# Merging the two rounds of the 32x32-tile transforms into one six-bank group, and kept sums in half banks

## The chip, the cores and the metric

The kernel runs on one core of a Trainium2 chip: TensorE (PE, with its weight loads listed apart as PEld), VectorE (DVE), ScalarE (ACT), GpSimd (POOL) and SyncE (SP, whose work here is to issue DMAs), with eight PSUM banks of 128 partitions x 512 float32 values between TensorE and the others. The metric is the time of one execution on the device in microseconds, the median of several runs.

## The reference

The input x has 2048 rows of 640 values (bfloat16). It is normalised row by row; the normalised rows go two ways, through a filter in the frequency domain and through a two-layer perceptron, and both results are added to x:

```
xn  = (x - mean(x)) / sqrt(var(x) + 1e-5)          # per row
F   = irfft2(rfft2(xn) * (w_r + i*w_i))            # 2048 x 321 weights
M   = gelu(xn @ w1 + b1) @ w2 + b2                 # 640 -> 1536 -> 640
out = x + F + M
```

## The kernel before

Everything is matrix multiplication on TensorE, the Fourier transforms too: a two-dimensional transform is cut into short transforms that are products with small constant tables (gtab, etab, mtab on the way in, ntab, getab, htab on the way out).

**The filter's way.** x is loaded as 16 chunks of 128 rows, normalised, and turned (chunks 0 to 3 by TensorE, 4 to 15 by transposing DMAs on SP) into xnT. Stage A multiplies folded rows with gtab, the b groups multiply with etab and leave Xb. Stage **C** finishes the forward transform along the rows with products of 32x32: for each P of 0 to 3 (two pairs of row blocks), two rounds r, each of 32 matmuls of 32x322 (Xb with mtab). The sixteen 32x32 tiles of the array work side by side, each on its own 32 rows and 32 columns; the two halves v = 0, 1 (real and imaginary) are accumulated on each other. A round fills four banks, which two copies of 644 columns empty into Y, one for each pair. DVE multiplies Y with the weights (L841, T<-Y,Wf) and adds the parts (L845, Z<-T). Stage **D** goes back: for each P, two rounds v, each of 32 matmuls of 32x320 (Z with ntab) into four banks. Each pair's two banks are emptied by a copy of 512 and one of 128 columns, which read PSUM at every second column and write U. Transposing DMAs (L866) turn U into XV again; stage E (getab) and the last products (htab) follow, with unfolding adds on DVE between them (L896, L901).

**The perceptron's way.** The first layer (xnT,W1, listed as xnT,W) is worked in six blocks of chunks, twelve column blocks of w1 each; ACT applies gelu (L774) into gT. The second layer (W2,gT, listed as W,gT) needs twelve products per chunk. For nine of the sixteen chunks (KEEP) these are made early: two banks collect twelve times 512 + 128 columns, and one DVE add of 640 (L948) puts them into an f32 store, which already holds b2 (L924) and x (an accumulating DMA on POOL, L942). At the end DVE adds the filter's result to it (L957) and the rows go out. The other chunks make the second layer at the end, in the same banks as the htab products.

**Order.** The sequence of operations on every engine is written out in a table (ORDER, one list of operation numbers per engine). Within an engine the program runs in that order; an engine waits by semaphores for results of others, and TensorE doesn't wait for itself: sync() leaves those waits out (`d.eng != o.eng or o.eng != "pe"`). ZONE says in which of the eight PSUM banks each kind of product may be put; a group can start when all of its banks have been emptied. So between two groups of C or D, TensorE works on first- and second-layer matmuls in the banks left over. All matmuls are issued by one helper, so they have the line L550; ACT's copies have L561 and DVE's L562, after the helper `copy`. The groups are told apart by their operands.

## Time and profile before

| | us |
|---|---|
| median of 3 runs | 146.68 (146.58 to 147.81) |
| span of the profiled execution, first to last instruction | 144.9 |
| TensorE busy in it | 141.2 |
| VectorE busy | 112.2 |
| ScalarE busy | 79.5 |
| GpSimd busy | 23.8 |

Beside the span no time is listed for the whole of the profiled execution; the runs' median lies 1.8 us above the span. In a row of the profile, "L550 PE MATMUL ps<-Xb,mtab 32*32 32x322 bf16 x32" is 32 matmuls of line 550 on TensorE in tiles of 32x32, with 322 columns each. In the timeline the first number is the start in us from the span's start, the second the time from the first start to the last end of the row's instructions; what stands in brackets is the idle time of the engine before the row and what ended it. In the groups of instructions the two numbers behind the first bar are the total busy time in us and the mean length of one in ns; lengths of pipelined matmuls overlap each other.

### The profile page before, as it was taken

Reading aid. Unit: us, or ns where it says so; the run is one execution under the profiler, and the core shown is the slowest. Engines: PE = TensorE matmul, PEld = TensorE weight load, DVE = VectorE, ACT = ScalarE, POOL = GpSimd, SP = SyncE. Lnnn points to the kernel's source line nnn. Section 1 sums busy time; section 2 is a strip of 40 time slices with the busy share of each in tenths; the row PEclk is TensorE's granted clock in tenths of the full one; section 3 lists DMA queues with packets and bytes.
Section 4 is the critical chain, followed back from the end, with each engine's and each line's share of the span. In section 5 each row is a group of like instructions: output and inputs, shape, how many; then the busy total and the mean of one; then the engine's idle time right before and its main releaser. Section 6 shows DMA issues by size and latency. Waiting matters only on the chain.

```text
span 144.9 us, 4085 instructions
## 1 busy us (share of the span) xinstructions
PE 141.2 (97%) x1720; PEld 90.6 (63%) x1720; DVE 112.2 (77%) x235; ACT 79.5 (55%) x145; POOL 23.8 (16%) x40
## 2 busy tenths in 40 slices
PE   7899999999999999999999999999999999999994
PEld 7799998987455464457554645554446666656573
DVE  1999999999843459799866967992432998998984
ACT  3219999999989668762455633216376755201000
POOL 2331302206100018220200120000054700000000
DMA  4998998987999736948767561362459895103225
GB/s 117 340 410 321 339 164 255 160 146 202 212 301 168 186 59 129 241 104 170 153 179 127 59 144 42 46 142 59 91 112 216 180 209 187 52 5 136 93 106 165
DMA packets 30841, 23.63 MB, mean 163 GB/s; under 512 B 20456, under 2 KB 26856, under 8 KB 30696
## 3 DMA queue, kind: packets, MB, share of 16 engines
q1 hardware_dynamic: 28432, 17.81, 50.5%
q0 software_dynamic: 2368, 5.57, 17.7%
q8 instruction: 13, 0.21, 0.6%
q14 instruction: 4, 0.03, 0.1%
q10 hardware_dynamic: 24, 0.00, 0.0%
HBM read 13.54 MB, written 2.62 MB: 112 GB/s over the span
## 4 chain that ended last, share of the span: by engine, by line
PE 94%; DMA 2%; DVE 2%; issue 0%; ACT 0%
PE ps L550 94%; DMA X<-in_A_x_dram 2%; DVE stats L670 1%; PE ps L714 1%; DVE mv L672 0%; ACT xnT L561 0%; DVE W L957 0%; DVE T L695 0%
## 5 line engine op out<-in xcount | busy, mean ns | idle before, releaser
L550 PE MATMUL ps<-W,gT 128*128 128x512 bf16 (+3 forms) x396 | 58.7, 295 | 0.0
L550 PE MATMUL ps<-xnT,W 128*128 128x256 bf16 (+2 forms) x384 | 58.4, 300 | 0.1
L550 PEld LDWEIGHTS ps<-W,gT 128*128 128x128 bf16 x396 | 30.3, 98 | 23.5 <-issue 1.6
L550 PEld LDWEIGHTS ps<-xnT,W 128*128 128x128 bf16 x384 | 33.3, 98 | 15.7 <-issue 1.6
L774 ACT ACTIVATE gT<-ps,b1col 128x256 bf16<-128x256 f32 (+1 forms) x72 | 35.4, 558 | 6.9 <-PE ps L550 6.5
L670 DVE BATCH_NORM_STATS2 stats<-X 128x6 f32<-128x320 bf16 x32 | 13.9, 476 | 2.1 <-DMA X<-in_A_x_dram 2.1
L561 ACT ACTIVATE Wf<-ps 128x960 bf16<-128x960 f32 (+1 forms) x8 | 7.0, 901 | 13.5 <-PE ps L550 13.5
L942 POOL DMA_DIRECT2D X<-in_A_x_dram x8 | 7.1, 1100 | 39.7 <-DMA Wf<-in_A_w_r_dram 17.1
L841 DVE TENSOR_TENSOR T<-Y,Wf 128x1288 bf16<-128x1288 bf16 x16 | 12.7, 826 | 0.0
L942 POOL DMA_DIRECT2D xnT<-in_A_x_dram x8 | 7.6, 1193 | 25.1 <-ACT xnT L924 25.1
L674 POOL TENSOR_TENSOR rstd<-mv,mhalf 128x2 f32<-128x2 f32 (+1 forms) x10 | 7.1, 714 | 26.6 <-DVE mv L672 26.4
L562 DVE CAST Y<-ps 128x644 bf16<-128x644 f32 x8 | 6.5, 828 | 5.5 <-PE ps L550 5.5
L561 ACT ACTIVATE Xb<-ps 128x960 bf16<-128x960 f32 (+1 forms) x7 | 6.0, 857 | 7.3 <-PE ps L550 7.3
L561 ACT ACTIVATE XV<-ps 128x1280 bf16<-128x1280 f32 (+3 forms) x10 | 9.5, 963 | 0.7 <-PE ps L550 0.7
L562 DVE CAST Xb<-ps 128x960 bf16<-128x960 f32 (+1 forms) x5 | 5.5, 1092 | 4.3 <-PE ps L550 4.2
L730 DVE TENSOR_TENSOR T<-T 128x512 bf16<-128x512 bf16 (+1 forms) x32 | 8.5, 312 | 0.0
L695 DVE TENSOR_SCALAR T<-X,mv,rstd 128x640 bf16<-128x640 bf16 (+2 forms) x17 | 7.1, 430 | 0.9 <-POOL rstd L674 0.6
L896 DVE TENSOR_TENSOR Wf<-Wf 128x960 bf16<-128x960 bf16 (+1 forms) x12 | 7.0, 597 | 0.5 <-ACT Wf L561 0.3
L957 DVE TENSOR_TENSOR W<-ps,X 128x640 bf16<-128x640 f32 x8 | 6.5, 820 | 1.1 <-PE ps L550 1.1
L561 ACT ACTIVATE U<-ps 128x512 bf16<-128x512 f32 (+1 forms) x10 | 3.8, 434 | 6.2 <-PE ps L550 6.2
L845 DVE TENSOR_TENSOR Z<-T 128x644 bf16<-128x644 bf16 x16 | 7.2, 489 | 0.1
L957 DVE TENSOR_TENSOR W<-ps,xnT 128x640 bf16<-128x640 f32 (+2 forms) x10 | 6.7, 686 | 0.7 <-PE ps L550 0.7
(55 smaller groups left out, 135.4 us busy)
## 6 DMA issues: line engine op xcount, KB each, us to landing
X<-in_A_x_dram POOLq DMA_DIRECT2D x8, 320.0 KB, 5.2
xnT<-in_A_x_dram POOLq DMA_DIRECT2D x8, 320.0 KB, 5.1
out_dram<-W SPq DMA_DIRECT2D x15, 160.0 KB, 1.8
X<-in_A_x_dram SPq DMA_DIRECT2D x7, 320.0 KB, 6.7
W<-in_B_w_dram SPq DMA_DIRECT2D x5, 384.0 KB, 5.2
W<-in_B_w_dram SPq DMA_DIRECT2D x4, 480.0 KB, 7.2
Wf<-in_A_w_i_dram SPq DMA_DIRECT2D x6, 160.5 KB, 5.4
Wf<-in_A_w_r_dram SPq DMA_DIRECT2D x6, 160.5 KB, 4.0
```

The costliest lines, as they stand in the source:

```text
L550: ins = e.matmul(o_, lhsT=lw, rhs=rh, start=st, stop=sp_, skip_group_check=True)
L561: return e.activation(dst(), src(), ACT.Copy, scale=scale)
L562: return e.tensor_copy(dst(), src())
L670: st_op[c] = K.op([("dve", 0.393)], pr, lambda e, _, c=c, h=h: e.bn_stats(stats[:, c, 6 * h:6 * h + 6], view(X, c * D + H2 * h, [[1, H2]]) ...
L674: K.op([("pool", 0.65)], 500, lambda e, _, a=a, b=b: e.tensor_tensor(out=rstd[:, a:b], in0=mv[:, a:b, 1], in1=mhalf[:, a:b], op=ALU.pow), ...
L695: o = K.op([("dve", 0.066 + (d1 - d0) / 1980.0)], pr, lambda e, _, c=c, n=n, xnv=xnv, d0=d0, d1=d1: e.tensor_scalar(out=xnv(n, d0, [[1, d1 ...
L730: ring_ops.append(K.op([("dve", dve_us(4 * w, 2))], pr, lambda e, _, op=op, x1v=x1v, xfv=xfv, o_=o_, o0=o0, o1=o1, w=w: e.tensor_tensor(ou ...
L774: K.op([("act", act_us(128 * nt, 1))], pr + PRIO["gelu"] + GP[bi], lambda e, _, c0=c0, nt=nt, fc=fc, hps=hps, at=at: e.activation(gT[:, fc ...
L841: filt_ops.append(K.op([("dve", dve_us(4 * KP, 2))], pr, lambda e, _, k=k, Y=Y, TB=TB, pair=pair: e.tensor_tensor(out=view(TT, TB.slot * 8 ...
L845: K.op([("dve", dve_us(2 * KP, 2))], pr, lambda e, _, TB=TB, Z=Z, r=r, op=op: e.tensor_tensor(out=view(Zb, Z.slot * 4 * KP + r * KP, [[2 * ...
L942: xo_ops[c] = K.op([("pool", 0.9)], 51 - c / 20, lambda e, _, c=c, xov=xov: e.dma_start(xov(0, D), xv[:, c, :], accum_op=ALU.add), reads=[ ...
L957: K.op([("dve", dve_us(w))], 95, lambda e, _, os_=os_, fps=fps, o0=o0, w=w, xov=xov, base=base: e.tensor_tensor(out=view(W1, OST + os_.slo ...
```

## The change

1. **C:** both rounds of a P are one group of six banks. It is issued as three lists of 24, 48 and 24 matmuls (64 of 161 columns and 32 of 322). The second list follows the first at once. The third writes into the banks 0 and 1 again, behind what the first list put there, and so its first instruction waits on a semaphore until the first list is through (`hard`: the one case in which TensorE waits for itself). Three copies empty the group: 644 columns (of both pairs), 966 and 966.
2. **D:** both rounds of a P are one group of six banks, 128 matmuls of 32x160 in lists of 32, 64 and 32, the third waiting as above. The moving operand is every second element of Z, so that the result stands contiguously in PSUM. The group is emptied in three operations: 256 + 64 columns for each of the two pairs, 768 + 192 for the second pair, and 768 + 192 for the first.
3. **Kept sums:** in two halves of 320 columns, each in one bank, with twelve matmuls of 320 and a DVE add of 320 each.
4. **Banks and order:** ZONE gives C and D the banks 0 to 5 or 2 to 7, the first layer prefers banks 6 and 7, then 4 and 5. The table ORDER is new on every engine.

The number of columns that TensorE streams in C, D and the second layer is the same as before. The core of the diff, without the tables:

```diff
--- before.py
+++ after.py
...
-        o.alts, o.alt = alts, None
+        o.alts, o.alt, o.hard = alts, None, ()
-            o.waits = [d for d in set(o.deps) if d.nbytes or d.eng != o.eng or o.eng != "pe"]
+            o.waits = [d for d in set(o.deps) if d.nbytes or d.eng != o.eng or o.eng != "pe" or d in o.hard]
...
-ZONE = {"hps": [(4, 8)], "bps": [(0, 4)], "cps": [(0, 4)], "dps": [(0, 4)],
-        "eps": [(0, 4)], "fin": [(4, 8), (0, 4)], "fps": [(4, 8)], "tps": ANY, "aps": ANY}
+ZONE = {"hps": [(6, 8), (4, 6), (0, 4)], "bps": [(0, 4), (4, 8)], "cps": [(0, 6), (2, 8)], "dps": [(0, 6), (2, 8)],
+        "eps": [(0, 4), (4, 8)], "fin": [(4, 8), (0, 4)], "fps": [(6, 8), (4, 6), (0, 4)], "tps": ANY, "aps": ANY}
-CHAIN = "b1 b0 c01 c00 b2 c10 d01 c11 d00 b4 b3 d10 d11 c20 c21 b5 c30 d20 d21 c31 d30 d31".split()
+CHAIN = "b1 b0 c0 b2 c1 d0 b4 b3 d1 c2 b5 c3 d2 d3".split()
...
+        def chained(lists, prio, reads, ps):
+
+            a = pe([("small", 0.147)], prio, lists[0], reads=reads, writes=[ps])
+            b = pe([("small", 0.294)], prio + 5, lists[1], reads=reads, writes=[ps], gate=[a])
+            c = pe([("small", 0.188)], prio + 6, lists[2], reads=reads, writes=[ps], gate=[b], after=[a])
+            c.hard = [a]
+            return c
+
...
-            for r in range(2):
-                cps = Buf(f"cps{P}_{r}", psum, 4, ZONE["cps"])
-                zone[f"c{P}{r}"] = pe([("small", 0.335)], PRIO["pc"] - P / 2 + 0.02 * r, lambda P=P, r=r, cps=cps: [
-                    (psb(cps.slot + 2 * pp + hi, [[1, KP]], 0, 64 * qq + 32 * (lo ^ pp), 32),
-                     part(mtab, 64 * hi + 32 * lo, 32, (P == pp == qq == hi == lo == 0) * 128 + v * 64 + r * 32, [[1, 32]]),
-                     part(xb3, 64 * hi + 32 * lo, 32, xb_at[4 * P + 2 * pp + qq]() + v * KP, [[1, KP]]), v == 0, v == 1)
-                    for v in range(2) for pp, qq, hi, lo in tiles],
-                    reads=in_xb + [B_xbpad, B_m], writes=[cps])
-                for pp, Y in enumerate(Ys):
-                    K.op([("act", act_us(644)), ("dve", dve_us(644))], PRIO["pc"] - two[pp] / 5,
-                         copy(lambda Y=Y, r=r: view(Yb, Y.slot * 4 * KP + r * KP, [[2 * KP, 2], [1, KP]]),
-                              lambda cps=cps, pp=pp: psb(cps.slot + 2 * pp, [[512, 2], [1, KP]])), reads=[cps], writes=[Y])
+            cps = Buf(f"cps{P}", psum, 6, ZONE["cps"])
+            KH = KP // 2
+
+            def ctile(pp, r, v, k0, k1, bank, at, P=P, cps=cps):
+                return [(psb(cps.slot + bank + hi, [[1, k1 - k0]], at, 64 * qq + 32 * (lo ^ pp), 32),
+                         part(mtab, 64 * hi + 32 * lo, 32, (P == pp == qq == hi == lo == 0) * 128 + v * 64 + r * 32, [[1, 32]]),
+                         part(xb3, 64 * hi + 32 * lo, 32, xb_at[4 * P + 2 * pp + qq]() + v * KP + k0, [[1, k1 - k0]]), v == at == 0, v == 1)
+                        for _, qq, hi, lo in tiles[:8]]
+            zone[f"c{P}"] = chained([
+                lambda t=ctile: t(0, 0, 0, 0, KH, 0, 0) + t(1, 0, 0, 0, KP, 2, 0) + t(0, 0, 1, 0, KH, 0, 0),
+                lambda t=ctile: t(0, 0, 0, KH, KP, 4, 0) + t(1, 0, 1, 0, KP, 2, 0) + t(0, 0, 1, KH, KP, 4, 0) + t(0, 1, 0, 0, KP, 4, KH) + t(1, 1, 0, 0, KH, 2, KP) + t(1, 1, 1, 0, KH, 2, KP),
+                lambda t=ctile: t(0, 1, 1, 0, KP, 4, KH) + t(1, 1, 0, KH, KP, 0, KH) + t(1, 1, 1, KH, KP, 0, KH)],
+                PRIO["pc"] - P / 2, in_xb + [B_xbpad, B_m], cps)
+            ya, yb = Ys
+            for n, bufs, dst, src in (
+                    (644, Ys, lambda ya=ya, yb=yb: view(Yb, ya.slot * 4 * KP, [[2 * KP, 2], [(yb.slot - ya.slot) * 4 * KP + KP + KH, 2], [1, KH]]), lambda cps=cps: psb(cps.slot, [[512, 2], [KH, 2], [1, KH]])),
+                    (966, [yb], lambda yb=yb: view(Yb, yb.slot * 4 * KP, [[2 * KP, 2], [1, KP + KH]]), lambda cps=cps: psb(cps.slot + 2, [[512, 2], [1, KP + KH]])),
+                    (966, [ya], lambda ya=ya: view(Yb, ya.slot * 4 * KP + KH, [[2 * KP, 2], [1, KP + KH]]), lambda cps=cps: psb(cps.slot + 4, [[512, 2], [1, KP + KH]]))):
+                K.op([("act", act_us(n)), ("dve", dve_us(n))], PRIO["pc"] - P / 2, copy(dst, src), reads=[cps], writes=bufs)
 
...
-            for v in range(2):
-                dps = Buf(f"dps{P}_{v}", psum, 4, ZONE["dps"])
-                d_ops.append(pe([("small", 0.335)], PRIO["ipc"] - P / 2 + 0.02 * (1 - v), lambda P=P, v=v, Zs=Zs, dps=dps: [
-                    (psb(dps.slot + 2 * pp + qq, [[1, H2]], 0, 64 * hi + 32 * lo, 32),
-                     part(ntab, 64 * qq + 32 * (lo ^ pp), 32, (P == pp == qq == hi == lo == 0) * 96 + 32 * ((0, 2), (1, 0))[v][r], [[1, 32]]),
-                     part(Zb, 64 * qq + 32 * (lo ^ pp), 32, Zs[pp].slot * 4 * KP + (2 * hi + r) * KP + v, [[1, H2]]), r == 0, r == 1)
-                    for r in range(2) for pp, qq, hi, lo in tiles], reads=Zs + [B_n], writes=[dps]))
-                zone[f"d{P}{v}"] = d_ops[-1]
-                for pp, U in enumerate(Us):
-                    def evac(e, name, U=U, v=v, uv=uv, dps=dps, pp=pp):
+            dps = Buf(f"dps{P}", psum, 6, ZONE["dps"])
+
+            def dtile(pp, q, r, bank, at, P=P, Zs=Zs, dps=dps):
+                return [(psb(dps.slot + bank + qq, [[1, Q4]], at * Q4, 64 * hi + 32 * lo, 32),
+                         part(ntab, 64 * qq + 32 * (lo ^ pp), 32, (P == pp == qq == hi == lo == 0) * 96 + 32 * ((0, 2), (1, 0))[q // 2][r], [[1, 32]]),
+                         part(Zb, 64 * qq + 32 * (lo ^ pp), 32, Zs[pp].slot * 4 * KP + (2 * hi + r) * KP + q // 2 + q % 2, [[2, Q4]]), r == at == 0, r == 1)
+                        for _, qq, hi, lo in tiles[:8]]
+            d_ops.append(chained([
+                lambda t=dtile: t(0, 0, 0, 0, 0) + t(1, 0, 0, 2, 0) + t(0, 0, 1, 0, 0) + t(1, 0, 1, 2, 0),
+                lambda t=dtile: [x for k in range(2) for r in range(2) for x in t(0, 1 + k, r, 4, k) + t(1, 1 + k, r, 2, 1 + k)],
+                lambda t=dtile: [x for r in range(2) for x in t(0, 3, r, 4, 2) + t(1, 3, r, 0, 1)]],
+                PRIO["ipc"] - P / 2, Zs + [B_n], dps))
+            zone[f"d{P}"] = d_ops[-1]
+            for own in ((0, 0), (1, 3)), ((1, 0),), ((0, 1),):
+                many = 3 if len(own) == 1 else 1
+
+                def evac(e, name, own=own, many=many, Us=Us, uv=uv, dps=dps):
+                    for pp, q in own:
                         for o_, w in ((0, 128), (512, 32)):
-                            ins = copy(lambda: uv(U, o_ + 2 * w * v, [[D, 2], [w, 2], [1, w]]), lambda: psb(dps.slot + 2 * pp, [[512, 2], [1, 2], [2, w]], o_ // 2))(e, name)
-                        return ins
-                    K.op([("act", act_us(512) + act_us(128)), ("dve", dve_us(512) + dve_us(128))], PRIO["ipc"] - two[pp] / 5, evac,
-                         reads=[dps], writes=[U, B_us[pp]], after=a_ops + ring_ops)
+                            ins = copy(lambda: uv(Us[pp], o_ + w * q, [[D, 2], [w, many], [1, w]]), lambda: psb(dps.slot + (0 if many == 1 else 4 - 2 * pp), [[512, 2], [Q4, many], [1, w]], o_ // 4 + Q4 * (q == 3)))(e, name)
+                    return ins
+                K.op([("act", len(own) * (act_us(256 * many) + act_us(64 * many))), ("dve", len(own) * (dve_us(256 * many) + dve_us(64 * many)))], PRIO["ipc"] - P / 2, evac,
+                     reads=[dps], writes=[x for pp, _ in own for x in (Us[pp], B_us[pp])], after=a_ops + ring_ops)
...
                 if kept:
-                    kps = Buf(f"kps{c}", psum, 2, ZONE["fps"])
-                    second(c, kps, 0, D, pr, ([kept_ops[-2]] if len(kept_ops) > 1 else []) + [l1_of[j][-1] for j, (t0, nt) in enumerate(BLOCKS) if t0 <= c < t0 + nt])
                     xo1, xo = xo, Buf(f"xk{c}")
-                    kept_ops.append(K.op([("dve", dve_us(D))], 30, lambda e, _, kps=kps, xov=xov: e.tensor_tensor(
-                        out=xov(0, D), in0=psb(kps.slot, [[1, D]]), in1=xov(0, D), op=ALU.add), reads=[kps, xo1], writes=[xo]))
+                    for o0 in (0, H2):
+                        kps = Buf(f"kps{c}_{o0}", psum, 1, ZONE["hps"])
+                        second(c, kps, o0, H2, pr, ([kept_ops[-2]] if len(kept_ops) > 1 else []) + [l1_of[j][-1] for j, (t0, nt) in enumerate(BLOCKS) if t0 <= c < t0 + nt], base=lambda o0: o0)
+                        kept_ops.append(K.op([("dve", dve_us(H2))], 30, lambda e, _, kps=kps, xov=xov, o0=o0: e.tensor_tensor(
+                            out=xov(o0, H2), in0=psb(kps.slot, [[1, H2]]), in1=xov(o0, H2), op=ALU.add), reads=[kps, xo1], writes=[xo]))
```

How the order stands now at three places. First, TensorE at the first group of C (Xb,mtab; etab,XV are the b groups, xnT,W1 the first layer, W2,gT the second). Before:

```order
L550 MATMUL ps<-xnT,W1 128x512 x5
L550 MATMUL ps<-Xb,mtab 32x322 x32
L550 MATMUL ps<-xnT,W1 128x512 x2
L550 MATMUL ps<-W2,gT 128x512
L550 MATMUL ps<-W2,gT 128x128
L550 MATMUL ps<-W2,gT 128x512
L550 MATMUL ps<-W2,gT 128x128
L550 MATMUL ps<-W2,gT 128x512
L550 MATMUL ps<-W2,gT 128x128
L550 MATMUL ps<-Xb,mtab 32x322 x32
L550 MATMUL ps<-xnT,W1 128x512 x3
```

The two rounds stand apart, with 2 first-layer matmuls and 3 pairs of the second layer between them. The same place in the changed kernel, from the second half of the first merged group to the b group that follows:

```order
L551 MATMUL ps<-Xb,mtab 32x161 x8
L551 MATMUL ps<-Xb,mtab 32x322 x8
L551 MATMUL ps<-Xb,mtab 32x161 x16
L551 MATMUL ps<-Xb,mtab 32x322 x8
L551 MATMUL ps<-Xb,mtab 32x161 x16
L551 MATMUL ps<-W2,gT 128x320 x3
L551 MATMUL ps<-xnT,W1 128x512 x5
L551 MATMUL ps<-W2,gT 128x320 x3
L551 MATMUL ps<-etab,XV 128x160 x24
```

The 64 matmuls of two rounds have become 96 narrower ones in one run (40 more of them stand ahead of these rows), and eleven matmuls stand between the group and the next b group.

Second, TensorE at the first group of D (Z,ntab) of the changed kernel:

```order
L551 MATMUL ps<-W2,gT 128x320 x15
L551 MATMUL ps<-xnT,W1 128x512 x10
L551 MATMUL ps<-Z,ntab 32x160 x128
L551 MATMUL ps<-W2,gT 128x320 x21
L551 MATMUL ps<-etab,XV 128x160 x24
```

Before, two groups `Z,ntab 32x320 x32` stood at different places there, with first- and second-layer matmuls and a group of C between them; now 128 matmuls stand in one run and 21 of the second layer behind them.

Third, the queue of POOL from the first rstd on (rstd is the scale of the normalisation, Wf the filter's weights). Before:

```order
L674 TENSOR_TENSOR rstd<-mv,mhalf 128x1 x2
L674 TENSOR_TENSOR rstd<-mv,mhalf 128x2 x3
L571 MEMSET Xb 128x6x3
L674 TENSOR_TENSOR rstd<-mv,mhalf 128x2 x2
L545 DMA Wf<-in_A_w_i_dram 16x5136
L674 TENSOR_TENSOR rstd<-mv,mhalf 128x2
L545 DMA Wf<-in_A_w_r_dram 16x5136
```

And now:

```order
L675 TENSOR_TENSOR rstd<-mv,mhalf 128x1
L574 MEMSET Wf 128x2
L675 TENSOR_TENSOR rstd<-mv,mhalf 128x1 x2
L546 DMA Wf<-in_A_w_i_dram 16x5136
L546 DMA Wf<-in_A_w_r_dram 16x5136
L675 TENSOR_TENSOR rstd<-mv,mhalf 128x2 x6
```

Both loads of filter weights have moved ahead of all six rstd of two chunks, and the clearing of Xb to the front of the program.

## The prediction

> **What bounds the kernel now.** First the page: how much of the span each engine works, and how evenly.

> ```profile
> span 144.9 us, 4085 instructions
> PE 141.2 (97%) x1720; PEld 90.6 (63%) x1720; DVE 112.2 (77%) x235; ACT 79.5 (55%) x145; POOL 23.8 (16%) x40
> PE   7899999999999999999999999999999999999994
> PE 94%; DMA 2%; DVE 2%; issue 0%; ACT 0%
> ```

> TensorE is busy for 97% of the span, in every slice but the first two and the last, and the chain that ended last is 94% TensorE. The chain of waits tells whether it is one unbroken run:

> ```profile
> 11.67 131.12 PE ps L550 x1598
> 142.78 0.02 issue
> 142.81 0.33 DVE W L957
> ```

> It is: from 11.67 to 142.78 us each matmul is released by the matmul before it. So only what changes the time of the matmul stream moves the end, or what opens a gap in it. Busy is not the same as streaming columns, though, so I look for matmuls that come apart further than their columns explain. The pitch first, from the timeline at two plain places:

> ```profile
> 108.07 1.79 PE L550 MATMUL ps<-W,gT 128*128 128x512 bf16 x12
> 109.70 0.59 PE L550 MATMUL ps<-xnT,W 128*128 128x512 bf16 x2
> ...
> 141.71 0.99 PE L550 MATMUL ps<-W,gT 128*128 128x160 bf16 x12
> 142.54 0.23 PE L550 MATMUL ps<-Wf,htab 128*128 128x160 bf16 x1
> ```

> Twelve matmuls (six of 512 and six of 128 columns) take 109.70 − 108.07 = 1.63 us, 0.272 for 640 columns, 0.425 ns a column; twelve of 160 columns take 0.83, 0.069 each, 0.43 ns a column. Now the timeline around one group of 32x32 tiles in C, then in D:

> ```profile
> 75.15 0.81 PE L550 MATMUL ps<-xnT,W 128*128 128x512 bf16 x3
> 75.89 0.19 PEld L550 LDWEIGHTS ps<-Xb,mtab 32*32 32x32 bf16 x32 [0.42 <-ACT gT L774]
> 75.89 0.49 PE L550 MATMUL ps<-Xb,mtab 32*32 32x322 bf16 x32
> 76.32 1.04 PE L550 MATMUL ps<-xnT,W 128*128 128x512 bf16 x4
> 76.50 0.71 ACT L561 ACTIVATE Y<-ps 128x644 bf16<-128x644 f32 x1 [1.08 <-PE ps L550]
> 76.50 0.83 DVE L562 CAST Y<-ps 128x644 bf16<-128x644 f32 x1 [0.32 <-PE ps L550]
> ```

> ```profile
> 99.20 0.38 PE L550 MATMUL ps<-xnT,W 128*128 128x512 bf16 x1
> 99.51 0.19 PEld L550 LDWEIGHTS ps<-Z,ntab 32*32 32x32 bf16 x32 [0.42 <-issue]
> 99.51 0.49 PE L550 MATMUL ps<-Z,ntab 32*32 32x320 bf16 x32
> 99.94 0.99 PE L550 MATMUL ps<-W,gT 128*128 128x512 bf16 x6
> ```

> A 512-column matmul takes 0.218. The three from 75.15 are through at 75.80, the next full one starts at 76.32: the group costs 0.52. In D, 99.20 + 0.22 to 99.94: 0.52 again. Columns explain 0.27 of that, since each tile streams two matmuls of 0.137 and the sixteen tiles run side by side. The rest is read with the length of one matmul:

> ```profile
> L550 PE MATMUL ps<-Xb,mtab 32*32 32x322 bf16 x256 | 4.0, 301 | 0.0
> L550 PE MATMUL ps<-Z,ntab 32*32 32x320 bf16 x256 | 3.9, 301 | 0.0
> L550 PEld LDWEIGHTS ps<-Xb,mtab 32*32 32x32 bf16 x256 | 1.5, 87 | 2.6 <-DVE Y L562 0.7 <-issue 0.5 <-ACT Xb L561 0.4
> ```

> The last matmul starts at 75.89 + 0.49 − 0.30 = 76.08. So entry costs 0.09 (75.80 to 75.89); first start to last start is 0.19, which is one pass of 0.14 and 0.05 by which the sixteen tiles are staggered; then 0.24 to the next full matmul, of which 0.14 are columns and 0.10 the way out. Some 0.24 of each 0.52 is entry, stagger and exit, and that is paid in 16 groups (256 matmuls of each kind, 32 a group). It is the only loss inside the stream.

> **The change part by part.**

> **One group for two rounds.** Columns stay the same: per tile four matmuls of 322 become 1288 columns in other cuts, 1280 in D. Eight pairs of groups become eight groups, so each pair pays 0.24 once instead of twice: 1.04 becomes 0.80. 8 x 0.24 = −1.9 us.

> **The new wait.** The last of three lists writes banks that the first list shares, and its first weight load waits until the first list's result is in. TensorE waits for itself, and everything behind it in program order waits too. The first list's last matmul starts one pass of 161 columns and the stagger after the group's first: 0.07 + 0.05 = 0.12. How long from a last start to a released instruction? 76.08 to ACT's copy at 76.50 is 0.42 with 0.137 of columns; with 0.069 it is 0.35. So the third list can start at 0.47. Unhindered it would start after 960 columns a tile, 0.41. Loss 0.06 per group, 0.5 in all. TensorE's release of itself is in no row. Bounds: nothing, if it is as quick as the 0.10 way out, and 0.24 − 0.06 more, if the wait empties the array and a second entry and exit are paid. I take 0.06. Net **−1.4**.

> **Narrow passes.** D now has eight passes of 160 columns, each with its own 32x32 weights. The loads last 87 ns and a pass 69, so a load that can't be hidden behind the pass before costs up to 0.09 per pass. 128-wide loads lasted 98 ns (row below) and the 160-column matmuls still came 69 apart, so I take nothing. The issue of instructions must keep up too: a pair of load and matmul every 0.069 / 16 = 4.3 ns. In the group above 32 loads start within 0.19 − 0.09 = 0.10 us, 3.3 ns apart, so 32 pairs are shown at that rate and 128 are not.

> [...]

> **D's strided read.** The moving operand is read at every second element, not contiguously. The nearest rows are weight loads of the same operand name, contiguous for etab and at a wide stride for getab:

> ```profile
> L550 PEld LDWEIGHTS ps<-getab,XV 128*128 128x128 bf16 x64 | 4.9, 145 | 0.8
> L550 PEld LDWEIGHTS ps<-etab,XV 128*128 128x128 bf16 x64 | 4.6, 98 | 1.1 <-DVE XV L562 0.3 <-ACT Y L561 0.2
> ```

> 145 against 98 is +48%, at a stride of 32 bytes where D's is 4. Ends: nothing, and half the rate, 8 x 0.069 = +0.55 per group or +2.2. I take nothing, as the stride is an eighth of that row's. [...]

> **Evacuation and banks.** A C pair left by four copies of 644, now by 644, 966 and 966; a D pair by eight small ones, now eight with fewer columns at a stretch, read contiguously. The columns are the same, and two engines do it. But six banks are held longer, and two are left for the work in between.

> ```profile
> L561 ACT ACTIVATE Xb<-ps 128x960 bf16<-128x960 f32 x4 | 3.9, 972 | 5.3 <-PE ps L550 5.2
> L562 DVE CAST Xb<-ps 128x960 bf16<-128x960 f32 x4 | 4.6, 1158 | 2.6 <-PE ps L550 2.5
> ```

> The first copy starts 0.18 after the next full matmul (76.32 to 76.50). ACT then needs 0.71 + 0.97 for the 644 and a 966, DVE 1.16 beside it: the banks are free about 1.86 later, against 0.18 + 0.83 = 1.0 before. After the first C the new order puts three second-layer matmuls of 320, five of 512 and three of 320 ahead of a b group that claims four banks: 6 x 0.136 + 5 x 0.218 = 1.9. That just covers it. After the first D stand 21 of 320, 2.9. I take 0.05 for the tight place.

> **Kept sums in halves.** PE: 640 columns in two matmuls either way, 0. DVE:

> ```profile
> 75.35 0.82 DVE L948 TENSOR_TENSOR X<-ps,X 128x640 f32<-128x640 f32 x1 [0.17 <-PE ps L550]
> 141.84 0.72 DVE L957 TENSOR_TENSOR W<-ps,xnT 128x320 bf16<-128x320 f32 x2 [0.17 <-PE ps L550]
> 60.00:75.00 15.00, 15.00 (x254) 8.64 (x253) 12.54 (x21) 7.90 (x16) 1.98 (x3) 1.00 0.75 167
> ```

> One add of 640 takes 0.82, two of 320 about as long. DVE has 2.5 of 15 us free where most of them stand, so they are hidden; with a full DVE they would delay filters and with them the D groups.

> **The filter loads on POOL.** Two direct loads move from behind the last but one and the last rstd (33.24 the first) to behind the fourth one-chunk rstd, ahead of all six two-chunk ones.

> ```profile
> 14.10 0.70 POOL L674 TENSOR_TENSOR rstd<-mv,mhalf 128x2 f32<-128x2 f32 x1 [4.27 <-DVE mv L672]
> 33.24 0.69 POOL L545 DMA_DIRECT2D Wf<-in_A_w_i_dram  x1
> 12.00:15.00 3.00, 3.00 (x31) 2.71 (x30) 3.00 (x11) 3.00 (x9) 0.70 (x1) 1.00 0.78 271
> ```

> POOL idles 4.27 us before that rstd, so 2 x 0.69 of issue fits there. The 2 x 164 KB meet x loads and transposes in a stretch with a DMA share of 0.78; at its 271 GB/s they are 1.2 us of traffic. If each byte delayed the xnT transposes and TensorE had no cover, that is +1.2; in the trace TensorE has no gap in these stretches (idle 0.0), so I take nothing. Nothing is won at 33 us either.

> **The start of E.** After the last D, its copies, four transposes on SP and a copy must land before E:

> ```profile
> 107.77 0.63 DVE L562 COPY Y<-XV 128x512 bf16<-128x512 bf16 x1 [2.19 <-DMA XV<-gtab]
> 109.92 0.77 PEld L550 LDWEIGHTS ps<-getab,XV 128*128 128x128 bf16 x8
> ```

> The copy ends at 108.40, E begins 1.5 later. Now 27 matmuls of 320 and 25 of 512 (9.1 us) stand between last D and E, where it took 110.13 − 99.94 = 10.2, and the group's three copies end some 0.5 later than two. Slack 1.5 − 1.1 − 0.5 = −0.1 to about 0.3 (the D group is also shorter). Take 0.05, at most 0.6.

> **Sum.** −1.9 + 0.5 + 0.05 + 0.05 = −1.3. The span 144.9 becomes 143.6. The runs' median, 146.68, lies 1.8 above that span, and nothing outside the span changes: **145.4**.

> **The rivals.**

> *The wait costs little* (no self-wait loss): −1.9, 144.8. For it: the way out, 0.10, is short. Against: 0.42 from last start to ACT.

> *Gaps at banks, the filter loads or E.* Up to 1.2: 145.7 to 146.7. For: slack near 0 at two places. Against: TensorE had none in the trace.

> *The change doesn't do what it says.* The mid-group wait empties the array and pays the switch again, 0.24 in place of 0.06, or the loads of narrow passes show, 0.09 in each of seven passes less what was saved: the gain is gone, 146.2 to 146.9. Against: the 128-wide rows.

> *Issue runs dry in groups beyond 64 instructions.* At 5 ns an instruction (1.5 times the 3.3 of a pair) D takes 256 x 5 + 0.24 = 1.5 and C 192 x 5 + 0.24 = 1.2, against 1.04: 4 x 0.46 + 4 x 0.16 = +2.5, 149.2; from 4 ns on it loses. For: no longer group in the trace. Against: 3.3 for a whole pair.

> *Slower: the strided read at half rate.* +2.2 on the sum: 147.6; the gain is used up at 1.6 times a pass. For: 145 against 98. Against: 32 bytes there, 4 here. At +48% it is 146.5.

> **How the numbers follow.** Forecast (145.0 to 145.7) 0.45; cheap wait (144.6 to 145.0) 0.13; gaps 0.17; wasted merge 0.07; strided read (146.5 to 147.8) 0.09; issue 0.06; more than one of these 0.03. The likeliest gives 145.4. Two in ten left out, the range reaches from 144.7 to 147.4, over the strided read's middle. 1% is about what a measurement of this kernel can tell from no change, 1.47 us: faster means under 145.2, which is the cheap wait and some 0.4 of the forecast, 0.32; slower means over 148.1, most of the issue rival and of the mixtures, 0.11; the rest 0.57.

> **What would show it.** Around a merged group in the timeline: 0.85 to 0.9 from natural end to the next full matmul; the third list's loads released by PE itself, some 0.06 late. D's last 32 matmuls against C's tell stride apart. PE idle after the first C (b group), before E, and between 15 and 23 us should stay under 0.1. Wrong if DVE idle falls to nothing between 60 and 100 us, or matmuls in a group come further apart than 69 ns a pass.

## The result: slower by 4.7%

| | before | changed |
|---|---|---|
| median, us | 146.7 (146.58 to 147.81, 4 runs) | 154.09 (152.87 to 154.69, 4 runs) |
| ratio | | 1.047 (95% interval 1.042 to 1.053) |
| span of the profiled execution, us | 144.9 | 151.5 |
| TensorE busy, us | 141.2 | 144.8 |
| matmuls on TensorE (and as many weight loads) | 1720 | 2104 |

The prediction was 145.4, with a range to 147.4: a gain was forecast, and it is a loss. The profiled run is the shortest of the four (152.87); why the others are 0.8 to 1.8 us longer no trace of theirs shows, but the gaps read below differ in length from run to run. The page of the changed kernel, its head, the slices of TensorE and the chain by engine:

```profile
span 151.5 us, 4864 instructions
PE 144.8 (96%) x2104; PEld 100.2 (66%) x2104; DVE 110.3 (73%) x243; ACT 82.8 (55%) x142; POOL 23.4 (15%) x40
PE   7899999999999999999969999999969999999994
PE 65%; DMA 15%; SPq 7%; DVE 5%; ACT 4%; issue 2%; POOL 0%; DVEq 0%
```

Two things have changed at once. TensorE does the same columns but is busy 3.6 us longer; and two slices that were full now stand at 6, so there are gaps. The chain that was 94% TensorE is only 65% TensorE. The 6.6 us of the span are found at these places; each is read below.

| place | changed against before, us |
|---|---|
| merged groups: 4 of C and 4 of D against 16 (10.16 against 8.31) | +1.85 |
| a gap directly behind the second D group | +1.50 |
| a gap ahead of E | +1.40 |
| first to third pair of gtab products (15.80 to 23.01 against 15.33 to 21.47) | +1.07 |
| up to the first gtab pair (15.80 against 15.33) | +0.47 |
| a kept sum that waits for its accumulating DMA, at 68 us | +0.25 |
| sum of these | +6.54 |

The fifth row isn't the change's: unmerged kernels of the experiments below, with the early order of before, come to the first pair at 15.81 and 15.93.

**The groups.** The timeline around the second group of C and the first of D (start, time to the last end, instructions; a row names its first form only, so the 96 matmuls of C are 64 of 161 columns and 32 of 322):

```profile
56.30 0.57 PE L551 MATMUL ps<-W,gT 128*128 128x320 bf16 x3
56.80 1.13 PE L551 MATMUL ps<-Xb,mtab 32*32 32x161 bf16 x96
57.87 0.39 PEld L551 LDWEIGHTS ps<-W,gT 128*128 128x128 bf16 x4
...
61.65 0.59 PE L551 MATMUL ps<-xnT,W 128*128 128x512 bf16 x2
62.17 1.17 PEld L551 LDWEIGHTS ps<-Z,ntab 32*32 32x32 bf16 x128 [0.42 <-ACT gT L775]
62.17 1.33 PE L551 MATMUL ps<-Z,ntab 32*32 32x160 bf16 x128
63.43 0.45 PE L551 MATMUL ps<-W,gT 128*128 128x320 bf16 x2
```

Three matmuls of 320 from 56.30 are through at 56.71, the next full one starts at 57.87: 1.16 for a merged C. Two of 512 from 61.65 are through at 62.09, the next starts at 63.43: 1.35 for a merged D. Two separate groups cost 1.04. The entry is as before (62.09 to 62.17), but the 128 loads, which would start within 0.42 us at the old 3.3 ns a pair, take 1.17 − 0.09 = 1.08, 8.5 ns a pair. The starts in the trace show how: 32 pairs at 3.3 ns, a pause of 0.13 us, then each further pair 8.3 ns behind the one before, through all three lists (one step of 34 ns in the middle apart). C has the same two rates, with a few more steps of 17 to 36 ns and, in three of its four groups, one of 64 to 103. Nothing stands out where the third list waits for the first.

**The gap behind the second D group:**

```profile
74.77 1.32 PE L551 MATMUL ps<-Z,ntab 32*32 32x160 bf16 x128
76.14 1.22 DVE L563 CAST T<-ps 128x768 bf16<-128x768 f32 x2 [1.09 <-PE ps L551]
77.53 0.58 PE L551 MATMUL ps<-W,gT 128*128 128x320 bf16 x3 [1.43 <-DVE T L563]
```

The profile names DVE's copy (to 77.36) as the releaser. The program doesn't bear that out: these three matmuls go into bank 7, outside the group, and wait for a kept add that had ended at 75.04. The copy only happens to end just before. What it was is settled by the runs.

**The gap ahead of E:**

```profile
109.00 2.99 ACT L562 ACTIVATE Y<-XV 128x1536 bf16<-128x1536 bf16 x1
110.75 0.63 DVE L563 COPY Y<-XV 128x512 bf16<-128x512 bf16 x1 [7.43 <-DMA XV<-T]
111.87 1.28 ACT L775 ACTIVATE gT<-ps,b1col 128x512 bf16<-128x512 f32 x2
112.67 0.54 PE L551 MATMUL ps<-getab,XV 128*128 128x160 bf16 x5 [1.24 <-DVE X L973]
```

The transposed rows are in place when DVE's copy ends, at 111.38, but E starts at 112.67. The profile names a kept add on DVE; by the program, E's first matmuls also wait for a bank that ACT's first gelu after 111.87 empties, and its semaphore comes at 112.58. That gelu stood behind a copy of 1536 columns which the new order gives to ACT, where it takes 2.99 us; before, DVE did it in 1.54.

**The first 23 us.** The gtab products, the transposes and the two rows that they wait for, before and then changed:

```profile
15.33 0.44 PE L550 MATMUL ps<-gtab,T 128*128 128x128 bf16 x5
18.73 0.72 PE L550 MATMUL ps<-gtab,T 128*128 128x128 bf16 x10
21.47 0.72 PE L550 MATMUL ps<-gtab,T 128*128 128x128 bf16 x10
15.31 5.32 SPq L702 DMA_TRANSPOSE xnT<-T  x4
```

```profile
15.80 0.44 PE L551 MATMUL ps<-gtab,T 128*128 128x128 bf16 x5
18.06 0.77 ACT L948 ACTIVATE X<-b2bc 128x640 f32<-128x640 bf16 x1
19.64 0.73 PE L551 MATMUL ps<-gtab,T 128*128 128x128 bf16 x10 [0.28 <-ACT XV L562]
21.80 0.50 DVE L671 BATCH_NORM_STATS2 stats<-X 128x6 f32<-128x320 bf16 x1 [0.78 <-DMA X<-in_A_x_dram]
23.01 0.73 PE L551 MATMUL ps<-gtab,T 128*128 128x128 bf16 x10 [0.17 <-DVE T L731]
15.64 6.81 SPq L703 DMA_TRANSPOSE xnT<-T  x4
```

Two things stand there that no part of the prediction priced, and one that it booked at nothing: on ACT the first kept chunk's bias (18.06) ahead of the copies that free banks for the second pair; on DVE the statistics of a later x chunk, which wait for its load, ahead of the folds of the third pair; and, beside the two filter loads, four transposes that take 6.81 us in place of 5.32.

### The profile page after: what moved, and what is told of

The parts are those of the page before. It is cut to its first block, busy times and chain, and to the rows that moved or that the text cites. A ratio compares the mean times of both kernels' runs of the same rounds, so it can differ in the third digit from the quotient of the medians.

```text
span 151.5 us, 4864 instructions
## 1 busy us (share of the span) xinstructions
PE 144.8 (96%) x2104; PEld 100.2 (66%) x2104; DVE 110.3 (73%) x243; ACT 82.8 (55%) x142; POOL 23.4 (15%) x40
## 4 chain that ended last, share of the span: by engine, by line
PE 65%; DMA 15%; SPq 7%; DVE 5%; ACT 4%; issue 2%; POOL 0%; DVEq 0%
PE ps L551 65%; DMA X<-in_A_x_dram 13%; SPq L546 5%; ACT Y L562 2%; DMA XV<-T 2%; DVE T L857 2%; SPq L890 2%; DVE T L563 1%; ACT U L562 1%; ACT T L562 1%; DVE X L973 1%; DVE stats L671 1%; ACT X L948 0%; DVE Y L563 0%; POOL X L966 0%
## 5 line engine op out<-in xcount | busy, mean ns | idle before, releaser
L551 PE MATMUL ps<-W,gT 128*128 128x320 bf16 (+3 forms) x396 | 58.9, 295 | 1.5 <-DVE T L563 1.4
L551 PEld LDWEIGHTS ps<-W,gT 128*128 128x128 bf16 x396 | 33.9, 98 | 21.5 <-DVE T L563 1.6
L551 PEld LDWEIGHTS ps<-xnT,W 128*128 128x128 bf16 x384 | 34.1, 98 | 15.3 <-ACT gT L775 0.5
L775 ACT ACTIVATE gT<-ps,b1col 128x256 bf16<-128x256 f32 (+1 forms) x72 | 34.9, 566 | 10.2 <-PE ps L551 10.0
L966 POOL DMA_DIRECT2D X<-in_A_x_dram x8 | 7.8, 1359 | 44.0 <-ACT X L948 24.5
L562 ACT ACTIVATE Wf<-ps 128x960 bf16<-128x960 f32 (+1 forms) x7 | 6.3, 931 | 11.8 <-PE ps L551 11.8
L973 DVE TENSOR_TENSOR X<-ps,X 128x320 f32<-128x320 f32 x16 | 7.6, 487 | 5.7 <-PE ps L551 3.3
L562 ACT ACTIVATE Xb<-ps 128x960 bf16<-128x960 f32 (+1 forms) x6 | 5.3, 884 | 8.8 <-PE ps L551 8.8
L562 ACT ACTIVATE XV<-ps 128x1280 bf16<-128x1280 f32 (+3 forms) x10 | 9.1, 936 | 1.1 <-PE ps L551 1.1
L562 ACT ACTIVATE Y<-ps 128x966 bf16<-128x966 f32 (+1 forms) x8 | 6.8, 907 | 4.8 <-PE ps L551 4.0
L562 ACT ACTIVATE U<-ps 128x768 bf16<-128x768 f32 (+3 forms) x10 | 4.6, 514 | 8.5 <-PE ps L551 8.5
L563 DVE CAST Xb<-ps 128x960 bf16<-128x960 f32 (+1 forms) x6 | 6.3, 1045 | 3.5 <-PE ps L551 3.5
```

Source lines behind the costliest of these rows:

```text
L551: ins = e.matmul(o_, lhsT=lw, rhs=rh, start=st, stop=sp_, skip_group_check=True)
L562: return e.activation(dst(), src(), ACT.Copy, scale=scale)
L563: return e.tensor_copy(dst(), src())
L775: K.op([("act", act_us(128 * nt, 1))], pr + PRIO["gelu"] + GP[bi], lambda e, _, c0=c0, nt=nt, fc=fc, hps=hps, at=at: e.activation(gT[:, fc ...
L966: xo_ops[c] = K.op([("pool", 0.9)], 51 - c / 20, lambda e, _, c=c, xov=xov: e.dma_start(xov(0, D), xv[:, c, :], accum_op=ALU.add), reads=[ ...
L973: kept_ops.append(K.op([("dve", dve_us(H2))], 30, lambda e, _, kps=kps, xov=xov, o0=o0: e.tensor_tensor(out=xov(o0, H2), in0=psb(kps.slot, ...
```

## The experiments

Two theories of the groups stood against each other. **Issue**: beyond the first 32 pairs TensorE doesn't get instructions faster than one pair in 8.3 ns, so narrow matmuls cost by their number. **Merge**: the strided read, the wait in the group or the six banks cost. For the gaps: **order** (who stands ahead of whom on ACT, DVE and POOL) against **place in the program** (where TensorE crosses from 256 instructions of its program to the next; the table of gaps below shows the 256).

### D read contiguously

```diff
-  Zs[pp].slot * 4 * KP + (2 * hi + r) * KP + q // 2 + q % 2, [[2, Q4]])
+  Zs[pp].slot * 4 * KP + (2 * hi + r) * KP + q // 2 + q % 2, [[1, Q4]])
```

> The changed kernel with D's moving operand read contiguously, so that D's results are not the reference's; nothing else changes. Issue theory: D stays at 1.35 us a group and the matmuls 8.3 ns apart, span 151.5. Rival (strided read at less than the full rate): D falls to about 1.0, span about 150.0.

Timeline of this kernel, at its second group of D, the matmuls behind it, and inside its last group of C:

```profile
75.28 1.17 PEld L551 LDWEIGHTS ps<-Z,ntab 32*32 32x32 bf16 x128 [0.21 <-issue]
75.28 1.32 PE L551 MATMUL ps<-Z,ntab 32*32 32x160 bf16 x128
79.19 0.58 PE L551 MATMUL ps<-W,gT 128*128 128x320 bf16 x3 [2.59 <-issue]
...
95.55 0.91 PE L551 MATMUL ps<-Xb,mtab 32*32 32x161 bf16 x67
97.45 0.39 PE L551 MATMUL ps<-Xb,mtab 32*32 32x161 bf16 x29 [0.99 <-issue]
```

The 128 loads take 1.17 and the matmuls 1.32, as with the stride, and the four groups cost 1.34 to 1.35: **the strided read costs this kernel nothing**. Since the pairs' pace could hide a slower read, look where it doesn't yet rule, in the first 32 pairs: the second pass of D starts 82 to 85 ns behind the first with the stride and 79 to 81 without, some 4 ns for 160 columns. The span was longer, 156.2, by gaps: the one behind the second D group is 2.59 us here, ends nowhere near DVE's copy, and the profile finds no releaser ("issue"). Another stands in the middle of a group of C, where no instruction waits for anything.

### The kernel before, with D's groups cut narrow

```diff
-  (psb(dps.slot + 2 * pp + qq, [[1, H2]], 0, ...),
+  (psb(dps.slot + 2 * pp + qq, [[1, Q4]], h * Q4, ...),
...
-  ... (2 * hi + r) * KP + v, [[1, H2]]), r == 0, r == 1)
-  for r in range(2) for pp, qq, hi, lo in tiles]
+  ... (2 * hi + r) * KP + v + h * Q4, [[1, Q4]]), r == h == 0, r == 1)
+  for h in range(2) for r in range(2) for pp, qq, hi, lo in tiles]
```

> The kernel before with each D group of 32 matmuls of 320 columns cut into 64 of 160, same columns, same banks, nothing merged, no wait added. Issue theory: the first 32 pairs as before, the other 32 at 8.3 ns a pair: 0.52 becomes about 0.8 us a group, eight groups, span 144.9 to 147.2. Rival (only the merge, its wait and its six banks cost): 0.52 a group, 144.9.

```profile
59.29 0.59 PE L550 MATMUL ps<-xnT,W 128*128 128x512 bf16 x2
59.81 0.61 PEld L550 LDWEIGHTS ps<-Z,ntab 32*32 32x32 bf16 x64 [0.42 <-DVE Z L845]
59.81 0.76 PE L550 MATMUL ps<-Z,ntab 32*32 32x160 bf16 x64
60.51 0.60 PE L550 MATMUL ps<-xnT,W 128*128 128x512 bf16 x2
```

From 59.29 + 0.44 to 60.51: 0.785, where the same columns in 32 matmuls took 0.52. The span grew from 144.9 to 147.6, 2.1 of it in the eight groups. No merge, no new wait, no new order: **narrowing alone costs 0.26 a group.**

### The kernel before, with D's wide matmuls issued twice

```diff
-  for r in range(2) for pp, qq, hi, lo in tiles]
+  for _ in range(2) for r in range(2) for pp, qq, hi, lo in tiles]
```

> The kernel before with each D group's 32 matmuls of 320 columns issued twice over (the second time they start the sums anew, so the results are the same): 64 load-and-matmul pairs a group, as in the narrowed kernel, but twice its columns. Issue theory (8.3 ns a pair from the 33rd on): first to last start about 0.52 as there, the group about 0.85 us. Column theory (time follows the columns): 0.52 + 0.27 = 0.79. Two wide rounds in one run would by either cost 0.8 to 0.85 in place of 1.04.

```profile
59.40 0.59 PE L550 MATMUL ps<-xnT,W 128*128 128x512 bf16 x2
59.93 0.90 PE L550 MATMUL ps<-Z,ntab 32*32 32x320 bf16 x64
60.76 0.61 PE L550 MATMUL ps<-xnT,W 128*128 128x512 bf16 x2
```

From 59.40 + 0.44 to 60.76: 0.92. That is more than either theory gave: with 320 columns the second pass starts later (146 to 148 ns behind the first in the kernel before, against 79 to 81 at 160 columns read contiguously), and the pause of 0.13 behind the 32nd pair comes on top (first to last start 0.60 against 0.52 in the narrow kernel). So twice the columns cost 0.14 more than the narrow group. And it sizes the best case of the idea: two wide rounds in one run would cost 0.92, not 0.80, against 1.04 apart. A merge can win 0.12 a pair, half of what the prediction booked.

### 80 matmuls a merged group

Three of a group's four pieces are whole, only one is cut; the second-layer halves, the six banks, the stride, the wait and the order are as in the changed kernel, and the copies that empty a group follow its pieces. C's part of the edit (D's is alike):

```diff
-  t(0, 0, 0, 0, KH, 0, 0) + t(1, 0, 0, 0, KP, 2, 0) + t(0, 0, 1, 0, KH, 0, 0),
...
+  t(0, 0, 0, 0, KP, 0, 0) + t(1, 0, 0, 0, KP, 2, 0) + t(0, 0, 1, 0, KP, 0, 0) + t(1, 0, 1, 0, KP, 2, 0),
+  t(0, 1, 0, 0, KP, 4, 0) + t(1, 1, 0, 0, KH, 2, KP) + t(0, 1, 1, 0, KP, 4, 0) + t(1, 1, 1, 0, KH, 2, KP),
+  t(1, 1, 0, KH, KP, 0, KP) + t(1, 1, 1, KH, KP, 0, KP)
```

> The changed kernel with fewer and wider matmuls in the merged groups, same banks, same columns, same results: three of the four pieces of a group whole (322 or 320 columns), only one cut in halves, so 80 matmuls a group instead of 96 (C) and 128 (D). D still reads every second element. Theory (beyond some 32 pairs TensorE gets a load and a matmul only every 8.3 ns): C falls from 1.16-1.24 to about 1.0, D from 1.35 to about 1.0 us a group, -2.2 in all, 151.9. Rival (the strided read or the wait inside the group is what costs): D stays near 1.35, C near 1.2, 154.

```profile
62.01 0.59 PE L551 MATMUL ps<-xnT,W 128*128 128x512 bf16 x2
62.53 1.05 PE L551 MATMUL ps<-Z,ntab 32*32 32x320 bf16 x80
63.51 0.99 PE L551 MATMUL ps<-W,gT 128*128 128x320 bf16 x6
```

From 62.45 to 63.51: D is 1.07, C 1.05 in the two groups that begin undisturbed (1.13 and 1.16 in the others). The median falls from 154.09 to 150.54 (1.025 of before, interval 1.019 to 1.030). The groups make up 1.5 us of the fall (10.16 to 8.67); besides, the gap behind the second D group is gone (1.50 in the first profile). D's stride shows here too: the second pass, of 320 columns, starts 154 to 157 ns behind the first, in C 146 to 148. The 0.92 of 64 wide pairs and 16 pairs more at 8.3 ns make 1.05, so little is left for the wait and the six banks to cost. And what is left of the merge is nothing: 1.05 to 1.07 against 1.04.

### The changed kernel again, and shifted by 64 instructions

No edit; and:

```diff
-WARM = (38, 0)
+WARM = (6, 0)
```

> The changed kernel once more, unedited. Theory (the gap behind the second D group is TensorE waiting for its next 256 instructions): a gap stands at the same place, of another length (1 to 3 us), and the groups cost the same to 0.05 us. Rival (a semaphore of DVE holds TensorE there): the gap ends each time just behind the DVE copy of 768 and 192 columns.

> The changed kernel with 6 instead of 38 warm-up matmuls at the start of TensorE's program, so that every later instruction stands 64 places earlier in it. Theory (gaps that no semaphore explains stand where TensorE crosses into the next 256 instructions of its program, if the 256 before went by faster than they can be fetched): the gap of 1.4 us directly behind the second D group goes, since the border now falls inside that group with slower instructions in the same 256; a gap may stand elsewhere, again at the border (place 193 of 256). Rival (banks or copies behind that D group): the gap stays at its place, 1.4.

In the repeat the span was 155.6, the groups without a gap inside as before (C 1.16 to 1.24, D 1.35). The gap behind the second D group was 2.31, a D group was cut in two by another, and a third (0.87) stood ahead of that group. The timeline of the first and the second D group's end, and the table by stretches behind the latter (busy time and number of PE, PEld, DVE, ACT and POOL, then the granted clock, DMA share and GB/s):

```profile
63.52 1.19 PE L551 MATMUL ps<-Z,ntab 32*32 32x160 bf16 x112
65.06 0.29 PE L551 MATMUL ps<-Z,ntab 32*32 32x160 bf16 x16 [0.35 <-issue]
...
77.74 1.22 DVE L563 CAST T<-ps 128x768 bf16<-128x768 f32 x2 [1.09 <-PE ps L551]
80.01 0.98 PE L551 MATMUL ps<-W,gT 128*128 128x320 bf16 x3 [2.31 <-issue]
```

```profile
80.00:83.00 3.00, 2.99 (x12) 1.79 (x13) 0.00 (x0) 1.40 (x3) 0.00 (x0) 0.51 0.00 0
83.00:86.00 3.00, 3.00 (x110) 2.04 (x108) 1.30 (x2) 1.28 (x3) 0.00 (x0) 1.00 0.42 71
```

In the shifted kernel nothing stands behind the second D group:

```profile
75.63 1.32 PE L551 MATMUL ps<-Z,ntab 32*32 32x160 bf16 x128
76.89 0.58 PE L551 MATMUL ps<-W,gT 128*128 128x320 bf16 x3
```

Counted in TensorE's recorded instructions, the gaps without a releaser stand ahead of those in the second column. (Left out is the gap ahead of E, which the profile of the shifted run lists without a releaser too: it is 1.39 to 1.40 in all five, and read above.)

| kernel | gap ahead of instruction (start-to-start, us) | from the landing of the block's packet to that instruction, us |
|---|---|---|
| changed, first profile | 2241 (1.67) | 1.31 |
| changed, again | 1473 (1.17), 1729 (0.59), 2241 (2.54) | 1.56, 1.62, 1.49 |
| D read contiguously | 2241 (2.82), 3009 (1.22) | 1.41, 1.27 |
| loads late (below) | 1473 (1.25), 2241 (1.35) | 1.58, 1.27 |
| shifted by 64 | 1729 (0.65); none behind the second D group | 1.50 |

1473, 1729, 2241 and 3009 are all 193 more than a multiple of 256, in five profiles whose gaps lie at different work: twice inside a group, three times between second-layer matmuls, four times behind the second D group, which is itself 256 instructions long and fills the space between two borders. Moved by 64 instructions, that group no longer ends at a border, and its gap is gone, as expected. The rival for this gap is out too: DVE's copy ended 1.05 us earlier in the repeat (77.74 + 1.22 against 80.01) and 1.3 earlier with D read contiguously. The page's row of the instruction queue (packets, MB, share) goes the same way, here changed and then before:

```profile
q8 instruction: 16, 0.26, 0.8%
q8 instruction: 13, 0.21, 0.6%
```

The traces also time the packets. The first sets off near the first border, the second near the second, and so on (3.6 us ahead of it to 5.0 behind it); each is read here as the block behind the next border. In the first profile the packet ahead of 2241 starts at 74.96 and has landed at 76.22; TensorE starts the last matmul of the group at 75.86 and goes on at 77.53. The last column of the table gives that distance for all nine gaps: 1.27 to 1.62 us. At the 171 other borders of the thirteen profiles, the first of each aside, TensorE went on 1.26 us or more behind the landing. So, as read here, it is the fetch that is late. A packet can set off late itself: in the two runs with a gap at 1473 it started 2.9 and 3.2 us behind the border before, in the first profile and with D read contiguously, without that gap, 0.0 and 0.1.

In the repeat the granted clock then fell to 0.51 for three microseconds, which by an estimate from that row adds some 1.5 us to the gap's 2.31. The shifted run's 158.0 has other losses that say nothing on this: a slower start (3.63 us of idle time behind the six warm-up matmuls, the first gtab pair at 16.45), and 2.8 us behind a late accumulating DMA.

### The filter loads back at the end of POOL's rstd

```diff
-  72 25 24 79 86 93 100 107 114 591
+  72 79 86 93 100 107 25 114 24 591
```

> The changed kernel with one edit: the two filter loads on POOL stand again where they stood before (after the fifth two-chunk rstd and after the sixth). Theory (the loads share the DMA engines with the x loads and the transposes from 12.9 us on): the third pair of gtab groups, at 23.0 us in the changed kernel and 21.5 before, comes back to about 21.5, the span falls by 1.3 to 1.5 (151.5 to about 150.1), the time from 154.1 to about 152.7. Rival (the early gaps come from the new order of DVE's queue): no change, 154.1, third pair at 23.0.

It came out the other way: 155.7 (1.059, interval 1.049 to 1.069). First to third gtab pair fell only from 7.21 to 6.89, not to 6.1. And the program places its products in banks by replaying the order with its own estimates, so this edit moved a first-layer product from bank 6 into bank 5, which the first D group needs. The list of what TensorE waited for from 40 to 70 us shows it, beside one of the gaps at a border:

```profile
PE ps L551 <- issue: 0.9, 1, 0.9
PE ps L551 <- ACT gT L775: 0.9, 1, 0.9
```

### Mending the order step by step

All with 80 matmuls a group. The edits: the first kept chunk's bias (operation 621) later on ACT; the 1536-column copy (581) from ACT to DVE; in the last two, the first 113 operations of DVE in the order of before; filter loads late in the first and the last.

```diff
-  act:  ... 313 621 134 136 ... 636 400 ... 448 457 581 454 ...
+  act:  ... 313 134 136 ... 636 621 400 ... 448 457 454 ...
-  dve:  ... 734 574 582 ...
+  dve:  ... 734 574 581 582 ...
```

> The changed kernel with four edits: 80 matmuls a merged group; the filter loads back at the end of POOL's rstd; the first kept chunk's bias on ACT (18.06 us there) moved to behind the first-layer blocks of 256 columns; the 1536-column copy before E moved from ACT, where it took 2.99 us, to DVE, where it took 1.54 before. Theory: groups 1.05 to 1.07, gap at 19 us gone (0.65), third gtab pair at 21.5, gap before E from 1.4 to under 0.3; span 149.2 - 0.65 - 0.6 - 1.1 = 146.8, time about 148.2. Rival (E waits for the transposes, not for ACT): gap before E stays above 1.

> The kernel with 80 matmuls a merged group, with two edits on ACT's queue alone: the first kept chunk's bias leaves the stretch at 18 us, and the 1536-column copy before E goes to DVE; the filter loads stay early. Theory (ACT's queue is behind the gap at 19 us, 0.65, and behind half of the gap before E, 1.34): first to third gtab pair 7.17 becomes 6.7 to 6.8, gap before E 0.6 to 0.7, no gap at 36 us and none ahead of the first D group, span 149.2 to about 148.0, time about 149.3. Rival (the gaps follow from late x loads and transposes alone): both gaps stay, 150.5.

> The kernel with 80 matmuls a group and the two edits on ACT's queue, and the first 113 operations of DVE's queue again in the order of the kernel before (there the statistics of later x chunks stand behind the folds for the next gtab products, here ahead of some); the filter loads stay early. Theory (DVE waits for an x load with the folds queued behind it): first to third gtab pair falls from 7.7 in the run with the ACT edits alone to 6.3 to 6.6. Rival (the x loads and transposes are late whatever DVE's order): it stays above 6.9.

> The same with the filter loads at the end of POOL's rstd too, so that ACT, DVE and POOL do the first 20 us as in the kernel before. Theory: first to third gtab pair 6.1 to 6.3, as before (6.14); the difference to the run with early loads, 0.1 to 0.4, is what the loads cost by themselves. Rival (bank places of the first layer): above 6.5.

| edits on top of 80 a group | first to second gtab pair | first to third | first pair to first C | span | median (ratio, interval) |
|---|---|---|---|---|---|
| none | 3.85 | 7.17 | 35.36 | 149.2 | 150.54 (1.025, 1.019 to 1.030) |
| ACT, loads late | 3.40 | 6.49 | 35.90 | 150.2 | 150.86 (1.028, 1.024 to 1.031) |
| ACT | 3.40 | 7.73 | 36.29 | 149.8 | 151.12 (1.028, 1.024 to 1.031) |
| ACT, DVE | 3.40 | 6.26 | 35.60 | 149.8 | 150.81 (1.022, 1.003 to 1.041) |
| ACT, DVE, loads late | 3.40 | 6.26 | 34.12 | 147.6 | 149.57 (1.014, 0.994 to 1.033) |

The last two rows rest on two runs each. The bias on ACT costs 0.45 between the first two pairs, every time. With it gone alone, DVE's blocking is seen; the timeline of that third kernel:

```profile
20.09 0.76 DVE L731 TENSOR_TENSOR T<-T 128x512 bf16<-128x512 bf16 x2
22.31 0.49 DVE L671 BATCH_NORM_STATS2 stats<-X 128x6 f32<-128x320 bf16 x1 [1.47 <-DMA X<-in_A_x_dram]
22.72 0.21 DVE L731 TENSOR_TENSOR T<-T 128x128 bf16<-128x128 bf16 x1
```

Statistics wait 1.47 us for an x load, with the last 0.2 us of a fold, for which TensorE waits, behind them. With DVE's old order the third pair is at 6.26 (6.14 before), and there the place of the filter loads makes no difference. At the first C it does: 35.60 against 34.12, 1.5 us. With the loads early the four transposes take 6.58 us, with the loads late 5.51; but what TensorE waits for is ACT, 0.76 ahead of 24.37 us and 0.35 ahead of C, and the two programs differ in their bank places as well: with the loads early the last first-layer product ahead of C stands in bank 5, which C needs, with the loads late in bank 6. So 1.5 is what the edit is worth, and how much of it is the traffic of the loads isn't shown. The time doesn't fall with any smaller set of these edits that was run (DVE alone wasn't): what one gives is taken by the next. Only with all three does the first C move forward by 1.2, from 35.36 to 34.12.

Ahead of E, DVE's copy shortens the gap: 1.34 becomes 0.67 in the first mended kernel, 0.92 and 0.68 in the next two, and 0.3 in the last; the transposes' landing is the rest. In the last kernel TensorE's waits from 40 to 70 us hold the 0.9 at the bank place alone. Without that, by an estimate, it would come to about 146.6 of span, still 1.7 above 144.9. None of these is shown to beat the kernel before.

## Why the prediction was wrong

1. **Bound: right.** TensorE was the bound, the loss in entry, stagger and exit is real (the entry of 0.09 is in every run), and the columns of the changed kernel are the same.
2. **"Narrow passes": the step that failed.** It was booked at nothing, from "32 loads start within 0.10 us, 3.3 ns apart", with the remark that 128 pairs were not shown. The 3.3 ns hold for the first 32 pairs, 64 instructions, in every longer group too; from then on a pair takes 8.3 ns, not the 4.3 that a pass of sixteen narrow tiles needs. Narrowing alone cost 0.26 for 64 pairs in the kernel before, and the merged groups came to +1.85 where −1.9 + 0.5 was booked. The row read was of a burst, and a burst's rate was taken for a lasting one.
3. **The rival on issue** had the number right ("from 4 ns on it loses"; measured 4.15 an instruction, though that it is the issue is not shown) but a chance of 0.06, for no better reason than that the 32 pairs were fast. Its price mixes two units: 3.3 ns is for a pair, so 5 ns an instruction is three times as slow and not 1.5 times; and by its own formula the loss begins at 3.6 ns.
4. **The saving of the merge itself, 0.24 a pair:** at most 0.12, since the pause of 0.13 behind the 32nd pair comes inside the longer run (0.92 for 64 wide pairs). The rival of the wasted merge was also summed too low: 0.09 in each of seven passes of four D groups is 2.5, and so 147.9, not 146.9.
5. **The wait inside the group, 0.06:** not seen. At 8.3 ns a pair the second list lasts longer than the first list's way out: in all eight groups the semaphore of the first list comes 0.19 to 0.31 us before the third list starts.
6. **Strided read at nothing: right for the time**, 1.35 and 1.34, in part because the pairs' pace hides it (sixteen pairs at 8.3 ns are 133 ns, a strided pass of 160 columns 82 to 85). In the first 32 pairs it costs some 4 ns in a pass of 160 columns and 9 in one of 320, about 6%; half rate and +48% are out.
7. **Banks after the first C and D, 0.05:** no gap there in the changed kernel. The gap that looked like one, behind the second D group, is at a border of the program. That the program's own fetch can be late was no rival at all: 1.5 us in the first profile, more in the repeat.
8. **E, 0.05 and at most 0.6:** 1.40. The step counted the transposes, which came late about as reckoned (their copy ended at 111.38, TensorE was free at 111.27), and left out that the copy behind them had moved from DVE (1.54) to ACT (2.99), with the gelu that frees E's bank behind it.
9. **Filter loads on POOL, nothing:** right that POOL had room; but moving them back is worth 0.3 up to the third gtab pair of the changed kernel and 1.5 up to the first C where ACT and DVE are mended, above the bound of 1.2 (bank places included). The step looked at TensorE's idle time, which was zero, and not at how far x loads and transposes could slip before it was not.
10. **ACT's and DVE's new early order** was not priced at all. One bias ahead of two copies, where ACT was busy 3.00 of 3.00 us, cost 0.45.
11. **Kept sums in halves, nothing:** about right; the 0.25 at 68 us is a kept add behind its accumulating DMA.

What stays open: why the packet of a block sets off at once in some runs and up to 3 us late in others; what paces a pair at 8.3 ns (the issue of its two instructions or the load itself: in every run here each matmul has its own load, so they can't be told apart); and how much of the early loss belongs to each queue, since the edits don't add.

## What to carry to other kernels

A rate read from a short burst need not last (here 3.3 ns a pair became 8.3); before many small instructions replace few large ones, look in the trace for the longest run of them and price the rest by a bound from above. When a saturated engine's columns stay the same, count its instructions: two for each matmul here, 2104 matmuls and as many loads. And a new order for all engines is many edits: read each queue at the places where its engine is full, before the edit that gave the change its name.

## What the runs showed of the hardware

- 32x32 load-and-matmul pairs on TensorE, in D: 32 of them 3.3 ns apart, a pause of 0.13 us, and mostly 8.3 ns a pair from then on, at 160 and 320 columns.
- Gaps of 0.6 to 2.8 us (start to start) on TensorE at 193 past a multiple of 256 recorded instructions, when 192 to 256 of the 256 before belonged to such pairs. They end 1.27 to 1.62 us behind the landing of the 16 KB instruction packet that is read here as that of the block behind the border.
- A granted clock of 0.51 for 3 us after a gap of 2.31 us, and 1.00 after the gap of 1.43 us. The mean over the execution was 0.989 with the gap of 2.31 and with the one of 2.59, and 1.000 with the one of 1.43.
- A bf16 moving operand at every second element: a pass of 160 columns starts 82 to 85 ns behind the one before in place of 79 to 81, one of 320 columns 154 to 157 in place of 146 to 148.
- A copy of 1536 columns out of XV took 2.99 us on ACT and 1.54 on DVE.
